# A decode kernel's wo rows over 16 DMA engines, and its value tiles taken four blocks at a time

## The chip, the core and the metric

The kernel runs on one core of one Trainium2 chip. The metric is the device time of one execution in microseconds (us); below 192.66 us is the median of three runs (192.44 to 192.67). A profile of one execution and its trace are at hand: for each engine (PE, the TensorE matmuls; PEld, its weight loads; DVE, VectorE; ACT, ScalarE; POOL, GpSimd; SP, SyncE, which here only issues DMAs) the start and length of each instruction, and for the DMA engines every packet and every semaphore increment.

## The reference

A gated mix of two branches over one token x of 512 numbers, all in bf16:

```
q = (x @ wq) as 32 heads of 128
scores = q . k_cache * 128**-0.5          # k_cache, v_cache: 32 heads x 4096 x 128
o = softmax(scores) @ v_cache
a = o (4096 numbers) @ wo                 # wo: 4096 x 512
h = relu(x @ w1 + b1) ** 2                # 1376 wide
b = h @ w2 + b2
g = sigmoid(sum(x * gate_w))
out = g * a + (1 - g) * b                 # 512 numbers
```

Each cache is 32 MiB, wq and wo 4 MiB each, w1 and w2 2.7 MiB together. Every byte is used once.

## The kernel before, in words

**Tiles.** Four heads make a tile of 4 MiB, [128 partitions x 128 blocks x 128]: 32 partitions for each head, 128 positions in a partition. There are 8 key tiles and 8 value tiles. A ring of five slots holds them; the list `LOADS` has their order (k0, k1, k2, v0, k3, v1, ... k7, v5, v6, m, v7), where m is a slot with w1, w2 and the last part of wo. SP issues the loads in that order on one queue; before each one `free` waits until the slot's old tile is used up. For a value tile this is a count on `s_pv`, one for each unit done.

**Units and steps.** A tile is worked through in four units, and all engines follow a common count of steps i = 0 to 31, one for each key unit (the loops at the end of each engine's program). In step i

- DVE multiplies 20 blocks of the key unit with q and sums them (`ttr`, line 734; 24 blocks in the last tile);
- PE transposes the other 12 blocks (`transposes`, line 516), ACT copies them out (`evac`, line 415), PE forms their scores (`scores`, line 529) one step later;
- at a tile's border ACT copies the scores of PE into S (`sc_copy`, line 422), DVE takes the maximum over each partition (`smax`, line 741), PE turns it (`max_rows`, line 536), DVE takes it over the head (`gmax`, lines 748 and 751), PE spreads it (`max_cols`, line 541), ACT forms the exponentials E (`exps`, line 434). DVE does `gmax` behind the products of the next unit; only at the border before the last tile (i = 28) it does it ahead of them.
- PE multiplies value units with E (`pv`). Which ones in which step stands in the table `PV`: unit i - 11 as a rule, from step 25 on two at a time, none in steps 28 and 29, the rest in steps 30 and 32 and after the loop. In a step they come behind the transposes and scores.

**Two forms of a value unit.** The narrow form (line 570) loads each of 32 value blocks as weights and multiplies with four columns of E: 32 matmuls, the result in the layout that is wanted. The wide form (line 562) loads 16 columns of E as weights and multiplies with four blocks (512 columns) at once: 8 matmuls. Its result is [16 x 512], of which the four diagonal 4 x 128 pieces are wanted; ACT copies it to `parts` (`parts_copy`, line 440), and PE adds the pieces to the tile's narrow result (line 576). `WIDE` says how many units of a tile are wide: three in tiles 0 to 2, none in the others.

**Norms.** `den`, `recip` and `norm` divide a group of heads (`GR`: 0 to 7, 8 to 15, 16 to 23, 24 to 27, 28 to 31) by its sums and write `onorm`. `norm` of the first two groups stands on DVE behind the products of steps 19 and 27.

**wo.** The first 28 heads' part of wo goes into W, where wq was, once q is formed (`started`): 112 rows of 32 KB (32 rows of wo each), placed on the partitions so that each DMA engine moves a chosen number of them. `FIRST` lists the rows that SP sends (three at a time), `RUNS` those that POOL sends; POOL's queue takes its engines from a cursor, and `turns` sends small dummy loads (`dm`) that move it. By these lists engines 0, 1, 2, 4, 7 and 8 move eight rows, engine 3 one, the others seven. After the last norm of head 27, `turn_a` and `spread_a` bring the outputs into W's order by the selection matrix `selA`, and `out_a` and DVE's `rows_v` multiply with W; `add_v` adds DVE's sum. The last four heads' part and w2's last rows come at the end of SP's queue (`out_b`, `mlp_out`).

Of the kernel before, what the change touches and what calls it, by code (L numbers as in the profile page):

```python
# [5 lines left out]
def bass_gated_mix__gqa_block_cached__dense_activation_squared_relu__decode_kernel(  # L6
# [15 lines left out]
    fp32 = mybir.dt.float32  # L22
# [30 lines left out]
    PV = {i: [i - LAG] for i in range(LAG, LAG + (NT - 3) * U)}  # L53
    PV[25] = [14, 15]
    PV[26] = [16, 17]
    PV[27] = [18, 19]
    for i in (28, 29, 30):
        del PV[i]
    PV[NU - 2] = [NU - 3 * U, NU - 3 * U + 1]
    PV[NU] = list(range(NU - 3 * U + 2, NU - U))  # L60
# [4 lines left out]
    NG = len(GR)  # L65

    WIDE = {0: 3, 1: 3, 2: 3}
    SLOTS = 5
    NS = 2  # L70
    NC = 2
# [3 lines left out]

    NA = 28
    NZ = NH - NA
    TS = [0, 3, NZ]

    TV = 10  # L80
# [2 lines left out]
    INNER, OUTER, SEAM = range(3)  # L83
    RUNS = [(INNER, 4, 12, 0, 2), (INNER, 4, 12, 1, 2),
            (OUTER, 4, 4, 0, 1), (OUTER, 8, 8, 0, 1), (OUTER, 4, 4, 1, 1), (OUTER, 8, 8, 1, 1),
            (OUTER, 4, 4, 2, 1), (OUTER, 8, 8, 2, 1),
            (OUTER, 3, 2, 3, 1), (SEAM, 7, 2, 3, 1)]
    FIRST = [(INNER, 0, 3, 0, 1), (INNER, 0, 3, 1, 1), (INNER, 0, 3, 2, 1), (INNER, 0, 3, 3, 1),
             (OUTER, 0, 3, 0, 1), (OUTER, 0, 3, 1, 1), (OUTER, 0, 3, 2, 1), (OUTER, 0, 3, 3, 1)]

# [15 lines left out]
    def strips():  # L106
        q = 0
        for run in RUNS + FIRST:
            yield (*place(*run), q)
            q += place(*run)[2]  # L110
        assert q == 4 * NA

    STRIPS = list(strips())

# [19 lines left out]
    with ctx:  # L134
# [11 lines left out]
        def held(kind, j=0):  # L146
            return ring[:, AT[kind, j] % SLOTS, :]
# [9 lines left out]
        W5 = W4 + NZ * DM  # L157
        wob_sb = held("m")[:, W4:W5].rearrange("p (h n) -> p h n", h=NZ)
        oA, fin4 = [held("m")[0:p, W5 + n * 128:W5 + n * 128 + 128] for n, p in enumerate((NA, 4))]
        vsum = held("k", NT - 1)[:, 0:2 * DM].bitcast(fp32)  # L160

# [23 lines left out]
        onesf = sb("onesf", [128, 128], fp32)  # L186
        qcol = sb("qcol", [128, NH], bf16)
        S = sb("S", [128, NS, B], fp32)
        parts = sb("parts", [4 * R, 512], fp32)
        E = sb("E", [128, NE, B, R], bf16)  # L190
        mp = sb("mp", [128, NT], fp32)
        gm = sb("gm", [1, 2, R], fp32)
# [35 lines left out]
        acc = pQ[:, 256:260]  # L228

        def O(a, b):  # L230
            return [pO, pO, pX, pO, pX][[n for n, g in enumerate(GR) if g[0] <= a < g[1]][0]][:, 64 + a:64 + b]

        s_x = sem("s_x")
        s_wq = sem("s_wq")
# [7 lines left out]
        s_dm = [sem(f"s_dm{n}") for n in range(len(RUNS))]  # L242
        s_wr = sem("s_wr")
        s_wk = sem("s_wk")
        s_vl = {(j, n): sem(f"s_vl{j}{n}") for j in PARTS for n in range(len(PARTS[j]) - 1)}
        s_sel = sem("s_sel")
        s_b1 = sem("s_b1")
# [29 lines left out]
        s_e = sem("s_e")  # L277
        s_pv = sem("s_pv")
        s_pt = sem("s_pt")
        s_den = sem("s_den")  # L280
        s_rd = sem("s_rd")
        s_on = sem("s_on")
# [35 lines left out]
        @block.sync  # L318
        def _(eng):
            for n, (kind, j) in enumerate(LOADS):  # L320
                free(eng, n)
                if n == SLOTS - 1:
                    started(eng)
                    for p, st, k, q in STRIPS[len(RUNS):]:
                        eng.dma_start(W[p:p + st * (k - 1) + 1:st, :], woa_v[q:q + k, :]).then_inc(s_wr, 16)
                if kind == "v" and j in PARTS:
                    for w in range(len(PARTS[j]) - 1):
                        part = slice(PARTS[j][w] * 128, PARTS[j][w + 1] * 128)
                        eng.dma_start(held("v", j)[:, part], v_v[j][:, part]).then_inc(s_vl[j, w], 16)  # L329
                elif kind in "kv":  # L330
                    eng.dma_start(held(kind, j), (k_v if kind == "k" else v_v)[j])\
                       .then_inc(s_l[n % SLOTS], 16)
                elif kind == "m":
                    eng.dma_start(held("m")[:, 0:W2], w1_v).then_inc(s_w[0], 16)
                    eng.dma_start(held("m")[:, W2:W3], w2_v).then_inc(s_w[1], 16)
            for c in range(len(TS) - 1):
                eng.dma_start(wob_sb[:, TS[c]:TS[c + 1], :], wob_v[:, TS[c]:TS[c + 1], :])\
                   .then_inc(s_wo[c], 16)
            eng.dma_start(w2b, B_w2[F - 128:F, :]).then_inc(s_w[2], 16)
            eng.wait_ge(s_f4, 1)  # L340
            eng.dma_start(out[0, 0, :].rearrange("(j p) -> j p", p=128), fin4).then_inc(s_out, 16)

        @block.gpsimd
        def _(eng):
            eng.memset(ident[:, :], 0.0).then_inc(s_id, 1)
            eng.memset(identf[:, :], 0.0).then_inc(s_id, 1)
            eng.memset(onesf[:, :], 1.0).then_inc(s_cst, 1)
            eng.wait_ge(s_id, 2)
            for m in (ident, identf):  # L350
                eng.affine_select(out=m[:, :], in_=m[:, :], compare_op=ALU.not_equal, fill=1.0,
                                  base=0, pattern=[[-1, 128]], channel_multiplier=1)\
                   .then_inc(s_id, 1)
            eng.memset(RS[:, :], 0.0).then_inc(s_cst, 1)
            eng.memset(E[:, :, :, :], 0.0).then_inc(s_cst, 1)
            eng.memset(selA[:, :, :], 0.0).then_inc(s_sel, 1)
            eng.wait_ge(s_sel, 1)
            for n, (p, st, k, q) in enumerate(STRIPS):
                eng.wait_ge(s_sel, n + 1)
                part = selA[:, :, p:p + st * (k - 1) + 1]  # L360
                eng.affine_select(out=part, in_=part, compare_op=ALU.not_equal, fill=1.0, base=-st * q,
                                  pattern=[[st, 4], [-1, st * (k - 1) + 1]], channel_multiplier=4 * st)\
                   .then_inc(s_sel, 1)

            started(eng)
            sent = 0
            for n, ((back, d), run) in enumerate(zip(turns(), RUNS)):
                if back:
                    eng.inc_swdge_sem([], [], mode="reset_dge_cursor")  # L370
                if d:
                    src = B_w1[0:d, 0:32].rearrange("p (a c) -> p a c", a=2)
                    eng.dma_start(dm[0:d, sent, :, 0:4], src[:, :, 0:4]).then_inc(s_dm[sent], 16)
                    sent += 1
                p, st, k, q = STRIPS[n]
                eng.dma_start(W[p:p + st * (k - 1) + 1:st, :], woa_v[q:q + k, :],
                              max_dma_last_dim=16384).then_inc(s_wp[n], 16)
            for n in range(sent):
                eng.wait_ge(s_dm[n], 16)
            eng.wait_ge(s_wr, 16 * len(FIRST))  # L380
            for q in s_wp[:-1]:
                eng.wait_ge(q, 16)
            eng.wait_ge(s_wp[-1], 16)
            eng.memset(tick[:, :], 0.0).then_inc(s_wk, 1)
# [3 lines left out]
        def _(eng):  # L388
# [48 lines left out]

            def parts_copy(j):
                eng.wait_ge(s_pv, U * j + WIDE[j])
                eng.activation(parts[:, :], pX[0:4 * R, :], ACT.Copy).then_inc(s_pt, 1)  # L440

            for c in range(EARLY):
                qb_copy(c)
# [17 lines left out]
        def _(eng):  # L461
# [76 lines left out]
            def max_cols(j):  # L538
# [2 lines left out]
                eng.matmul(MB[:, j:j + 1], gx[0:1, j % 2, :], onesf[0:1, 0:1],  # L541
                           start=True, stop=True).then_inc(s_mb, 1)

            def pv(u):
                j, w = u // U, u % U
                lo, hi = w * B // U, (w + 1) * B // U
# [6 lines left out]
                    landed(eng, "v", j)  # L553
                if w == 0:
                    eng.wait_ge(s_e, R * (j + 1))
                    for g in range(2, NG):
                        if u == GR[g][0]:
                            eng.wait_ge(s_on, g - 1)
                n = WIDE.get(j, 0)
                if w < n:  # L560
                    for b in range(lo, hi, 4):
# [2 lines left out]
                                        start=(b == 0), stop=(b == n * B // U - 4), skip_group_check=True)  # L564
                    mm.then_inc(s_pv, 1)
                    return
                if n and w == n and R * j == GR[1][0]:
                    eng.wait_ge(s_on, 1)
                for b in range(lo, hi):
                    mm = eng.matmul(O(R * j, R * j + R), held("v", j)[:, b * 128:(b + 1) * 128],  # L570
                                    E[:, j % NE, b, :], start=(b == n * B // U), stop=(n == 0 and b == B - 1),
                                    skip_group_check=True)
                if n and w == U - 1:
                    eng.wait_ge(s_pt, list(WIDE).index(j) + 1)
                    for b in range(4):
                        mm = eng.matmul(O(R * j, R * j + R), parts[:, b * 128:(b + 1) * 128],  # L576
                                        identf[0:4 * R, R * b:R * b + R], start=False, stop=(b == 3),
                                        skip_group_check=True)
                mm.then_inc(s_pv, 1)

            def den(c):
# [17 lines left out]
            def out_a():  # L599
                eng.wait_ge(s_ac, 2)  # L600
                for t in range(TP):
                    for j in range(4):
                        eng.matmul(acc[:, j:j + 1], wo_sb[:, t, j * 128:(j + 1) * 128], o2A[:, t:t + 1],
                                   start=(t == 0 and j == 0), stop=False, skip_group_check=True)

            def add_v():
                eng.wait_ge(s_vs, TV)
# [66 lines left out]
            spread_a()  # L674
            out_a()
            max_cols(NT - 1)
            mlp_h()
            den(NG - 1)
            for n in range(FG):
# [14 lines left out]
        def _(eng):  # L694
# [65 lines left out]
            def norm(c):  # L760
                a, b = GR[c]
                eng.wait_ge(s_rd, c + 1)
                eng.wait_ge(s_pv, b)
                eng.scalar_tensor_tensor(out=onorm[:, a:b], in0=O(a, b), scalar=gcol[:, 0:1],
                                         in1=rden[:, a:b], op0=ALU.mult, op1=ALU.mult)\
                   .then_inc(s_on, 1)
# [39 lines left out]
            for i in range(NU + 1):  # L806
# [12 lines left out]
                    qcol_copy(EARLY + i - 1)  # L819
                if i >= 12 and (i - 12) % 8 == 0 and (i - 12) // 8 < NG - 2:  # L820
                    recip((i - 12) // 8)
                if i >= LAG + 1 and (i - LAG - 1) % 8 == 7 and i < NU:
                    norm((i - LAG - 1) // 8)
            norm(NG - 2)
            smax(NT - 1)
            eng.wait_ge(s_at, 1)
# [44 lines left out]
```

## Time and profile before

| | us |
|---|---|
| median of three runs | 192.66 |
| the profiled execution: time | 192.5 |
| its span, first to last instruction | 191.1 |
| DVE busy | 158.6 |
| PE busy | 122.1 |
| ACT busy | 84.3 |
| granted TensorE clock, mean over the span | 0.674 of full |
| moved by DMA | 78.70 MB, 412 GB/s over the span |

In the lines shown below, a line of the page's section 2 is the span in 40 slices, each digit a busy share in tenths. A line of groups has source line, engine, operation, output and inputs, count, then busy time in us, mean ns, and the idle time before it with what ended it. A line of a timeline has start (us from the span's start), length in us, engine, source line, operation, output and inputs, shapes and count, and in brackets the idle time ahead and what ended it. The matmuls of one line that follow each other are merged. In the page's table of queues, a line has packets, MB and share of the DMA engines' time; "instruction" queues carry the engines' own programs.

### The profile page before, as it was taken

The numbers are of one execution on the slowest core, as the hardware profiler recorded it, in microseconds if no ns is written. First come the engines' busy times: TensorE is split into PE (matmuls) and PEld (weight loads), VectorE is DVE, ScalarE is ACT, GpSimd is POOL, SyncE is SP. The second block draws the span as 40 slices with busy tenths as digits, with TensorE's granted clock in tenths as the row PEclk, the third lists the DMA queues.
The fourth block names the chain that finished last, engine by engine and source line by source line (L and its number), as shares of the span: only waits on it lengthen the run. The fifth ranks groups of instructions, "written<-read, shape, count | busy, mean of one in ns | idle before, by whom it ended". The sixth has DMA issues, their size and how long they took to land.

```text
span 191.1 us, 5609 instructions
## 1 busy us (share of the span) xinstructions
PE 122.1 (64%) x1864; PEld 92.8 (49%) x1866; DVE 158.6 (83%) x1387; ACT 84.3 (44%) x207; POOL 18.4 (10%) x48
## 2 busy tenths in 40 slices
PE   0019764644524694898499986845876488548975
PEld 0014343534413543276256544745876277437964
DVE  0031399999999999999999999998999799998821
ACT  2013975825843654077409542943644293000400
POOL 7630000990000000000000000000000000000000
PEclk9999998555555558699859759955555555555555
DMA  6999999999999999999999999999999999999992
GB/s 219 440 440 439 439 439 430 439 398 451 432 424 405 432 406 432 442 420 439 442 427 422 425 434 425 417 424 432 425 430 435 398 424 406 419 421 426 414 388 72
DMA packets 5298, 78.70 MB, mean 412 GB/s; under 512 B 1099, under 2 KB 1741, under 8 KB 1870
## 3 DMA queue, kind: packets, MB, share of 16 engines
q1 hardware_dynamic: 4488, 75.47, 93.1%
q0 software_dynamic: 768, 2.89, 3.7%
q8 instruction: 14, 0.23, 0.5%
q14 instruction: 14, 0.11, 0.2%
q10 hardware_dynamic: 14, 0.01, 0.0%
HBM read 78.35 MB, written 0.00 MB: 410 GB/s over the span
## 4 chain that ended last, share of the span: by engine, by line
DVE 46%; DMA 38%; SPq 7%; PE 4%; ACT 2%; issue 2%; DVEq 0%; ACTq 0%
DVE ring L734 43%; DMA ring<-in_A_k_cache_dram 25%; DMA ring<-in_A_wo_dram 14%; SPq L329 6%; DVE S L734 2%; PE pX L562 2%; ACT E L434 1%; PE KP L516 1%; PE pO L576 1%; ACT kT L415 0%; DVE gm L748 0%; DVE gx L751 0%; ACT parts L440 0%; PE pQ L637 0%; DVE mp L741 0%
## 5 line engine op out<-in xcount | busy, mean ns | idle before, releaser
L734 DVE CUSTOM_DVE_ANT_0 ring<-ring,qb 128x128 bf16<-128x128 bf16 x656 | 140.6, 281 | 1.4 <-DMA ring<-in_A_k_cache_dram 1.3
L415 ACT ACTIVATE kT<-KP 128x768 bf16<-128x768 bf16 (+1 forms) x64 | 46.6, 779 | 47.1 <-PE pQ L529 19.0
L734 DVE DVE_READ_ACCUMULATOR2_ANT S<- 128x1 f32 x656 | 50.5, 77 | 0.1
L516 PE MATMUL KP<-ident,ring 128*128 128x128 bf16 x368 | 37.9, 275 | 9.5 <-DMA ring<-in_A_k_cache_dram 6.2
L516 PEld LDWEIGHTS KP<-ident,ring 128*128 128x128 bf16 x368 | 30.9, 126 | 14.1 <-DMA ring<-in_A_k_cache_dram 6.5
L562 PE MATMUL pX<-ring,E 128*16 128x512 bf16 x72 | 24.0, 493 | 0.0
L434 ACT ACTIVATE E<-S,nM 32x128 bf16<-32x128 f32 x32 | 18.6, 580 | 1.0
L570 PE MATMUL pO<-E,ring 128*128 128x4 bf16 x352 | 10.8, 166 | 4.9 <-DMA ring<-in_A_v_cache_dram 4.9
L570 PEld LDWEIGHTS pO<-E,ring 128*128 128x128 bf16 x352 | 10.2, 102 | 5.3 <-DMA ring<-in_A_v_cache_dram 5.2
L536 PE MATMUL pM<-identf,mp 128*1 128x128 f32 x8 | 3.0, 370 | 15.1 <-DVE mp L741 15.1
L562 PEld LDWEIGHTS pX<-ring,E 128*16 128x16 bf16 x72 | 6.9, 106 | 11.5 <-issue 7.7
L570 PE MATMUL pX<-E,ring 128*128 128x4 bf16 x384 | 11.3, 166 | 1.6 <-DMA ring<-in_A_v_cache_dram 1.6
L570 PEld LDWEIGHTS pX<-E,ring 128*128 128x128 bf16 x384 | 11.0, 105 | 1.8 <-DMA ring<-in_A_v_cache_dram 1.8
L426 ACT ACTIVATE nM<-pM 128x1 f32<-128x1 f32 x8 | 1.4, 174 | 19.0 <-PE pM L541 19.0
L529 PE MATMUL pQ<-qcol,kT 128*128 128x4 bf16 x176 | 7.7, 168 | 2.3 <-ACT kT L415 2.3
L541 PE MATMUL pM<-onesf,gx 1*128 1x1 f32 x16 | 4.2, 329 | 7.0 <-DVE gx L751 7.0
L529 PEld LDWEIGHTS pQ<-qcol,kT 128*128 128x128 bf16 x176 | 7.1, 105 | 3.1 <-ACT kT L415 3.1
L536 PEld LDWEIGHTS pM<-identf,mp 128*1 128x1 f32 x8 | 0.7, 85 | 16.3 <-DVE mp L741 16.1
L700 DVE CUSTOM_DVE_ANT_0 ring<-ring 1x512 bf16<-1x512 bf16 x1 | 0.7, 680 | 9.4 <-DMA ring<-in_gate_w_dram 9.4
L529 PEld LDWEIGHTS pS<-qcol,kT 128*128 128x128 bf16 x192 | 7.4, 106 | 1.7 <-issue 1.7
L434 ACT ACTIVATION_READ_ACCUMULATOR E<-S,nM 32x1 f32 x32 | 8.1, 253 | 0.0
L529 PE MATMUL pS<-qcol,kT 128*128 128x4 bf16 x192 | 7.7, 168 | 0.0
(88 smaller groups left out, 109.0 us busy)
## 6 DMA issues: line engine op xcount, KB each, us to landing
ring<-in_A_k_cache_dram SPq DMA_DIRECT2D x8, 4096.0 KB, 29.5
ring<-in_A_v_cache_dram SPq DMA_DIRECT2D x5, 4096.0 KB, 29.0
W<-in_A_wq_dram SPq DMA_DIRECT2D x1, 4096.0 KB, 12.4
ring<-in_A_v_cache_dram SPq DMA_DIRECT2D x2, 2048.0 KB, 27.7
ring<-in_A_v_cache_dram SPq DMA_DIRECT2D x4, 1024.0 KB, 27.7
ring<-in_A_v_cache_dram SPq DMA_DIRECT2D x2, 1280.0 KB, 31.9
W<-in_A_wo_dram POOLq DMA_DIRECT2D x2, 768.0 KB, 17.9
ring<-in_B_w_dram SPq DMA_DIRECT2D x1, 1376.0 KB, 25.3
```

Of the source, the lines that this page charges most:

```text
L329: eng.dma_start(held("v", j)[:, part], v_v[j][:, part]).then_inc(s_vl[j, w], 16)
L415: eng.activation(kT[:, n % NC, 0:HB[u // U] * 128], KP[n % 3][:, 0:HB[u // U] * 128], ACT.Copy).then_inc(s_ev, 1)
L426: eng.activation(nM[:, j:j + 1], MB[:, j:j + 1], ACT.Copy).then_inc(s_nm, 1)
L434: eng.activation(E[rows, j % NE, :, r], S[rows, j % NS, :], ACT.Exp, bias=nM[rows, j:j + 1], scale=SCALE, accum_out=RS[rows, R * j + r:R * ...
L516: mm = eng.transpose(KP[n % 3][:, y * 128:(y + 1) * 128], held("k", j)[:, b * 128:(b + 1) * 128], ident[:, :])
L529: mm = eng.matmul(S2[j % 2][:, c:c + R], kT[:, n % NC, y * 128:(y + 1) * 128], qcol[:, R * j:R * j + R], start=True, stop=True)
L536: eng.transpose(MT[0:1, :], mp[:, j:j + 1], identf[:, :]).then_inc(s_mt, 1)
L541: eng.matmul(MB[:, j:j + 1], gx[0:1, j % 2, :], onesf[0:1, 0:1], start=True, stop=True).then_inc(s_mb, 1)
L562: mm = eng.matmul(pX[0:4 * R, :], E[:, j % NE, b:b + 4, :].rearrange("p b r -> p (b r)"), held("v", j)[:, b * 128:(b + 4) * 128], start=(b ...
L570: mm = eng.matmul(O(R * j, R * j + R), held("v", j)[:, b * 128:(b + 1) * 128], E[:, j % NE, b, :], start=(b == n * B // U), stop=(n == 0 a ...
L576: mm = eng.matmul(O(R * j, R * j + R), parts[:, b * 128:(b + 1) * 128], identf[0:4 * R, R * b:R * b + R], start=False, stop=(b == 3), skip ...
L734: ins = eng.tensor_tensor_reduce(kb, kb, qb[:, j, :], 1.0, 0.0, ALU.mult, ALU.add, S[:, j % NS, b:b + 1])
```

## The change

1. Two of the 112 rows (64 rows of wo) leave W. `FIRST` stays; `RUNS` is written so that engine 3 moves none, engines 11 to 15 six, all others eight. The 64 rows come instead as single rows of 1 KB onto 64 partitions of slot m, in one DMA on SP's queue ahead of w1, and `out_h` multiplies them with the last norm column.
2. Tiles 0, 1, 2 and 4 are wide in all four units, tile 3 in three: 19 of the 20 units of tiles 0 to 4.
3. The parts are handled otherwise: ACT copies the four pieces by four instructions to the partitions 0, 32, 64 and 96 of a zeroed [128 x 128] `parts`, and PE adds them by one matmul with a 0/1 matrix `wanted`, at the first unit of the next tile (`add_parts`). POOL makes both tensors at the start.
4. Units 18 and 19 no longer run together in step 27: 18 in step 27, 19 in step 28. The norms of the first two groups wait for one unit more where the tile is in `WIDE`, and stand one step later on DVE. All groups but the fourth now accumulate in the same PSUM bank, pO.

```diff
     PV[26] = [16, 17]
-    PV[27] = [18, 19]
-    for i in (28, 29, 30):
+    PV[27] = [18]
+    PV[28] = [19]
+    for i in (29, 30):
         del PV[i]
...
-    WIDE = {0: 3, 1: 3, 2: 3}
+    WIDE = {0: 4, 1: 4, 2: 4, 3: 3, 4: 4}
     SLOTS = 5
...
     NZ = NH - NA
+    HR = 64
     TS = [0, 3, NZ]
...
             (OUTER, 4, 4, 0, 1), (OUTER, 8, 8, 0, 1), (OUTER, 4, 4, 1, 1), (OUTER, 8, 8, 1, 1),
-            (OUTER, 4, 4, 2, 1), (OUTER, 8, 8, 2, 1),
-            (OUTER, 3, 2, 3, 1), (SEAM, 7, 2, 3, 1)]
+            (OUTER, 4, 4, 2, 1), (OUTER, 8, 3, 2, 1),
+            (OUTER, 4, 3, 3, 1), (SEAM, 7, 2, 3, 1), (OUTER, 9, 2, 3, 1)]
     FIRST = [(INNER, 0, 3, 0, 1), (INNER, 0, 3, 1, 1), (INNER, 0, 3, 2, 1), (INNER, 0, 3, 3, 1),
...
             q += place(*run)[2]
-        assert q == 4 * NA
+        assert q == 4 * NA - HR // 32
...
         oA, fin4 = [held("m")[0:p, W5 + n * 128:W5 + n * 128 + 128] for n, p in enumerate((NA, 4))]
+        woh_sb = held("m")[128 - HR:128, W5 + 256:W5 + 256 + DM]
         vsum = held("k", NT - 1)[:, 0:2 * DM].bitcast(fp32)
...
         S = sb("S", [128, NS, B], fp32)
-        parts = sb("parts", [4 * R, 512], fp32)
+        parts = sb("parts", [128, 128], fp32)
+        wanted = sb("wanted", [128, R], fp32)
         E = sb("E", [128, NE, B, R], bf16)
...
         def O(a, b):
-            return [pO, pO, pX, pO, pX][[n for n, g in enumerate(GR) if g[0] <= a < g[1]][0]][:, 64 + a:64 + b]
+            return (pX if GR[3][0] <= a < GR[3][1] else pO)[:, 64 + a:64 + b]
...
         s_wk = sem("s_wk")
+        s_wh = sem("s_wh")
         s_vl = {(j, n): sem(f"s_vl{j}{n}") for j in PARTS for n in range(len(PARTS[j]) - 1)}
...
         s_pt = sem("s_pt")
+        s_wt = sem("s_wt")
         s_den = sem("s_den")
...
                 elif kind == "m":
+                    eng.dma_start(woh_sb, A_wo[NA * 128 - HR:NA * 128, :]).then_inc(s_wh, 16)
                     eng.dma_start(held("m")[:, 0:W2], w1_v).then_inc(s_w[0], 16)
...
                    .then_inc(s_sel, 1)
+            eng.memset(parts[:, :], 0.0).then_inc(s_wt, 1)
+            eng.memset(wanted[:, :], 0.0).then_inc(s_wt, 1)
+            for b in range(4):
+                eng.wait_ge(s_wt, 2 + b)
+                eng.affine_select(out=wanted[:, :], in_=wanted[:, :], compare_op=ALU.not_equal, fill=1.0,
+                                  base=-(32 + R) * b, pattern=[[-1, R]], channel_multiplier=1).then_inc(s_wt, 1)
...
                 eng.wait_ge(s_pv, U * j + WIDE[j])
-                eng.activation(parts[:, :], pX[0:4 * R, :], ACT.Copy).then_inc(s_pt, 1)
+                if j == 0:
+                    eng.wait_ge(s_wt, 6)
+                for b in range(4):
+                    eng.activation(parts[32 * b:32 * b + 4 * R, :], pX[0:4 * R, b * 128:(b + 1) * 128], ACT.Copy)                       .then_inc(s_pt, 1)
...
+            def normed(j):
+                g = [n for n, g in enumerate(GR) if g[0] == R * j]
+                if g and g[0] not in (0, 3):
+                    eng.wait_ge(s_on, min(g[0], 3))
+            def add_parts(j):
+                eng.wait_ge(s_pt, 4 * (j + 1))
+                if WIDE[j] == U:
+                    normed(j)
+                eng.matmul(O(R * j, R * j + R), parts[:, :], wanted[:, :], start=(WIDE[j] == U), stop=True,
+                           skip_group_check=True)
             def pv(u):
...
                     eng.wait_ge(s_e, R * (j + 1))
-                    for g in range(2, NG):
-                        if u == GR[g][0]:
-                            eng.wait_ge(s_on, g - 1)
+                    if j - 1 in WIDE:
+                        add_parts(j - 1)
                 n = WIDE.get(j, 0)
...
                     return
-                if n and w == n and R * j == GR[1][0]:
-                    eng.wait_ge(s_on, 1)
+                if w == n:
+                    normed(j)
                 for b in range(lo, hi):
...
                                     skip_group_check=True)
-                if n and w == U - 1:
-                    eng.wait_ge(s_pt, list(WIDE).index(j) + 1)
-                    for b in range(4):
-                        mm = eng.matmul(O(R * j, R * j + R), parts[:, b * 128:(b + 1) * 128],
-                                        identf[0:4 * R, R * b:R * b + R], start=False, stop=(b == 3),
-                                        skip_group_check=True)
                 mm.then_inc(s_pv, 1)
...
                                    start=(t == 0 and j == 0), stop=False, skip_group_check=True)
+            def out_h():
+                eng.wait_ge(s_wh, 16)
+                for j in range(4):
+                    eng.matmul(acc[:, j:j + 1], woh_sb[:, j * 128:(j + 1) * 128], onorm[128 - HR:128, NA - 1:NA],
+                               start=False, stop=False, skip_group_check=True)
...
             max_cols(NT - 1)
+            out_h()
             mlp_h()
...
                 eng.wait_ge(s_rd, c + 1)
-                eng.wait_ge(s_pv, b)
+                eng.wait_ge(s_pv, b + (b // R - 1 in WIDE))
                 eng.scalar_tensor_tensor(out=onorm[:, a:b], in0=O(a, b), scalar=gcol[:, 0:1],
...
                     recip((i - 12) // 8)
-                if i >= LAG + 1 and (i - LAG - 1) % 8 == 7 and i < NU:
-                    norm((i - LAG - 1) // 8)
+                if i >= LAG + 2 and (i - LAG - 2) % 8 == 7 and i < NU:
+                    norm((i - LAG - 2) // 8)
             norm(NG - 2)
...
```

## The prediction

> **What bounds the kernel now.** The page was read first: the slices of DMA, of the granted TensorE clock and of PE, then the groups.
>
> ```profile
> PE   0019764644524694898499986845876488548975
> PEclk9999998555555558699859759955555555555555
> DMA  6999999999999999999999999999999999999992
> ...
> q8 instruction: 14, 0.23, 0.5%
> ...
> L734 DVE CUSTOM_DVE_ANT_0 ring<-ring,qb 128x128 bf16<-128x128 bf16 x656 | 140.6, 281 | 1.4 <-DMA ring<-in_A_k_cache_dram 1.3
> ```
>
> The 16 DMA engines are busy from 5 us to the last slice: transfers are the first bound. DVE, in its key products, has waited for a key tile 1.3 us in all: it is a second bound that the first hides by a hair. TensorE has the full clock only now and then, and none after 124 us. The q8 line is TensorE's own instructions, fetched in 14 packets of 16 KB by the same DMA engines.
>
> Next, the trace's semaphore increments, one for each DMA engine, show who finishes last. For the last load (w2b) they come at 185.7 (one engine), 186.6 to 187.3 (seven) and 188.3 to 188.8 (eight), mean 187.65. A 32 KB row takes an engine 1.22 us; a q8 packet took 0.97 to 1.10 us, in which its engine moved nothing else. So rows and instruction packets make the spread, and perfect balance is worth at most 188.8 - 187.65 = 1.15 us.
>
> Then the timeline of PE, where the value units run:
>
> ```profile
> 94.94 3.58 PE L562 MATMUL pX<-ring,E 128*16 128x512 bf16 x8
> ...
> 100.62 1.89 PE L562 MATMUL pX<-ring,E 128*16 128x512 bf16 x8
> ...
> 106.82 3.10 PE L562 MATMUL pX<-ring,E 128*16 128x512 bf16 x8
> ...
> 132.78 1.04 PE L570 MATMUL pO<-E,ring 128*128 128x4 bf16 x32
> ...
> 136.12 0.58 PE L541 MATMUL pM<-onesf,gx 1*128 1x1 f32 x2 [0.70 <-DVE gx L751]
> 136.64 1.87 PE L570 MATMUL pO<-E,ring 128*128 128x4 bf16 x64
> ...
> 141.08 1.87 PE L570 MATMUL pX<-E,ring 128*128 128x4 bf16 x64 [0.98 <-DMA ring<-in_A_v_cache_dram]
> ...
> 144.41 1.85 PE L570 MATMUL pX<-E,ring 128*128 128x4 bf16 x64
> 146.12 0.46 PE L529 MATMUL pS<-qcol,kT 128*128 128x4 bf16 x12
> ```
>
> A narrow unit (32 matmuls, L570) takes about 0.9 us at either clock. A wide one (8 matmuls of 512 columns, L562) takes 1.89 us at the full clock and 3.5 us at half. The wide form saves instructions and costs TensorE time. The last line is the last scores of key tile 6. What hangs on it is in the timeline of DVE:
>
> ```profile
> 148.92 0.28 DVE L741 TENSOR_REDUCE mp<-S 128x1 f32<-128x128 f32 x1
> 149.67 0.28 DVE L748 TENSOR_REDUCE gm<-pM 1x4 f32<-1x128 f32 x1 [0.47 <-PE pM L536]
> 149.99 0.21 DVE L751 TENSOR_SCALAR gx<-gm 1x128 f32<-1x128 f32 x1
> 150.84 0.29 DVE L734 CUSTOM_DVE_ANT_0 ring<-ring,qb 128x128 bf16<-128x128 bf16 x1 [0.65 <-DMA ring<-in_A_k_cache_dram]
> ```
>
> At this one tile border the maximum (L741 to L751) stands on DVE ahead of the next tile's products, not behind them. Scores that come late here stop DVE. And the end of PE's timeline:
>
> ```profile
> 184.41 1.21 PE L570 MATMUL pX<-E,ring 128*128 128x4 bf16 x40
> 186.27 1.44 PE L570 MATMUL pX<-E,ring 128*128 128x4 bf16 x48 [0.65 <-DMA ring<-in_A_v_cache_dram]
> 188.27 0.56 PE L637 MATMUL pQ<-onorm,ring 128*128 128x1 bf16 x16 [0.56 <-DMA ring<-in_A_wo_dram]
> ```
>
> PE waits 0.65 us there for the last value tile: the compute chain may be 0.65 us later before it moves the end.
>
> **The change part by part.** *Instructions.* Ten units turn from 32 matmuls to 8 (-240). The 24 matmuls that add the parts (12 in the code, two each) become 10, and the 64 single rows add 4. From 1864 matmuls that leaves 1614. The 14 packets came about every 129 weight loads; 1616/129 gives 12. Two packets less are 2 x 1.03 us on two of 16 engines.
>
> *Rows.* I joined the packets of an engine end to start. The engine that is last, 188.8, is then the one with a single row and DVE's instruction packets (8 KB, 0.33 us, and the packet behind each 0.65 us longer): engine 3. It loses its row, -1.22. Six engines got two q8 packets each, and five of them are, as I read it, 11 to 15: -1.22 each. Of engines 5, 6, 9 and 10 (+1.22), three ended near 187 and come to about 188.4; one may be the sixth that was hit twice, and loses one packet. One of engines 0 to 2 ended near 188.4 and keeps its eight rows. The single rows add four 1 KB packets to every engine, 42 ns apart at the end of the trace: +0.17. New last engine: 188.4 + 0.17 = 188.6. Gain 0.2 us; bounds: 1.15 (balance) and -0.2 (the engine near 188.64 keeps its place).
>
> *Hidden.* POOL gets two memsets (0.20 each), four selects and one more (0.28 to 0.43), ahead of its 21.65 us wait before L373. Its DMAs go from 7 dummies and 10 runs to 6 and 11, 0.6 us of issue each, ending at 43 us; the rows are needed at 172.87 (L595) and landed by 99.6. Without that cover the whole tail would wait for rows. SP issues one DMA more at 148.8, 0.4 us, and everything behind it 0.4 us later; the last value tile then waits for unit 19, which moves behind step 28, so its issue goes from 149.7 to about 156. Its data start near 177, 20 us of queue later. Were that gone, each us late would be a us of idle DMA. The first normalisation moves one step on, and waits for a unit that has run by then; the second (0.15 us) moves from before L741 to behind the 24 products of step 28, and unit 20 now waits for it. It is there at about 157.6; PE reaches unit 20 later.
>
> *Tiles 0 to 2.* The fourth unit goes from 0.95 us, a wait of 0.59 and 1.05 us of adding (86.79) to 1.89 and one two-pass matmul later, about 0.4. No loss; PE waits 2.1 to 2.7 us for DVE at those borders anyway.
>
> *Tiles 3 and 4* have no such cover. By starts, from PE's timeline:
> - Unit 13: 3.56 at half clock against 0.91: +2.65. The wait of 0.70 at L541 goes: unit 14 starts +1.95, at 138.6.
> - Unit 14 at full clock, as at 100.62: +1.0; transposes and scores behind it at full clock: -0.55 (0.68 against 1.23). PE is then at tile 4's door at 142.5. It was there at 140.1 and waited 0.98 for the value tile, so +1.4 of 141.08.
> - The parts of tile 3: ACT's exponentials end 1.95 later, at 141.3. Four copies follow; the row nearest to 16x128 is the exponential of 32x128, a next step after 0.33: 1.3 in all. PE waits till 142.7, adds 0.4: unit 16 starts at 143.1, +2.0. (Bounds for the copies: 0.59, the one copy of now, and 4 x 0.59.)
> - Units 16 and 17: 3.74 against 1.73: +4.0. Transposes -0.55. Unit 18 alone, 1.87, against 18 and 19, 1.71: +3.6.
>
> So the last scores of tile 6 start at 149.7. From their start to DVE's next product lie 1.38 (copies of S, ended 147.50) + 1.28 (148.92 to 150.20) + 0.04 = 2.7 us; the key tile allows 150.84, so 148.1 was allowed: DVE loses 1.6 us. At the end: +0.15 (the moved normalisation), -0.36 (DVE's wait at 172.0 for unit 27 goes), +0.12 (four more matmuls; 40 take 1.20 at L628), -0.65 (PE's wait for data). Sum +0.86. The DMA gain lies beside it and is lost.
>
> The profiled execution took 192.5 (span 191.1 and 1.4 around it), 0.16 under the median. 192.5 + 0.86 = 193.4.
>
> **A rule against the row.** Windows at 1.53 us modulo 3.41 hold every change of the granted clock in the trace, and the clock rose after windows filled to 80% or more by transposes and wide units. The window view has PE 8.90 us busy of the 10 from 136 to 146 at a granted clock of 0.50. *The Trainium skill, TensorE: Matmul & The Clock Gate, Part 1, has the clock come after one window of about 3.4 us of activity and go after an idle one. Taken by busy time it would have had PE at full clock here, which the 0.50 contradicts. That the windows run freely of the kernel, as it says, one trace can't show; it would spread the times of the runs.*
>
> **The rivals.** (1) Full clock from unit 13 on. Wide units cost 1.87 throughout and the transposes 0.55 less each; PE then waits for the parts till 140.8, and the scores start near 148.1, as allowed. DVE loses 0.1, its end stays inside the 0.65, and DMA decides: 192.5 - 0.2 = 192.3, no change to be told. For it: after the wide unit at 100.62 the clock stayed up for 4.9 us. Against: it falls in each gap like PE's 4.38 us wait at 131. *This is also what the skill's rule, taken by busy time, would give.* (2) The rows bite: as (1), but my engine in 0 to 2 is lighter than read, and the last landing nears the mean. PE's 0.65 caps it: 191.85 to 192.1, and it decides only if the scores start before 148.1. (3) The clock falls between units 14 and 16, in 3 us of light work, as it fell at 107.3 inside the unit at 106.82: units 16 to 18 lose up to 1.2 to 1.7, DVE 3.0: 192.5 + 2.3 = 194.8.
>
> **How the numbers follow.** Forecast case 0.40 (192.8 to 193.9 by the copies' bounds and window phase), rival (1) 0.25, (2) 0.20, (3) 0.15. Two runs of this kernel differ by about 0.2%, 0.39 us, without cause: a time from 192.27 to 193.05 is no change. Rival (2) is faster: 0.20. Rival (1) and the edge of the forecast case: 0.28. The rest, slower: 0.52. The range takes in (2)'s body and (3): 192.0 to 194.8.
>
> **What would show it.** q8 with 12 packets; 1614 matmuls; wide units at L562's new line near 3.5 once after 132 and 1.9 after; the scores before the border near 149.7 and DVE waiting on L741 for S or PE rather than for the key tile; the last products of DVE ending near 173; the last landing near 188.6 and PE not waiting for the last value tile. If DVE's product starts at 150.9 again, the step on units 13 to 18 is wrong; if the last landing moves over 0.5 us, the step on rows is.

## The result, and the profile after

| | before | after |
|---|---|---|
| median, us | 192.69 | 194.03 (193.85 to 194.66) |
| ratio | 1 | 1.0074 [1.0058, 1.0090] |
| the profiled execution, us | 192.5 | 194.06 |
| span, us | 191.1 | 192.7 |
| last landing of the last load (w2b), us | 188.80 | 190.36 |
| mean landing over the 16 engines, us | 187.65 | 187.84 |
| latest engine above the mean, us | 1.15 | 2.53 |

Slower by 0.74%, where +0.37% was forecast. The page of after, its slices, its queue of TensorE's instructions and the group of DVE's key products:

```profile
PE   0019765644524693898469866999699688749865
PEclk9999995755555558699996997599879785555555
DMA  6999999999999999999999999999999999999980
...
q8 instruction: 12, 0.20, 0.4%
...
L764 DVE CUSTOM_DVE_ANT_0 ring<-ring,qb 128x128 bf16<-128x128 bf16 x656 | 140.7, 282 | 0.6 <-DMA ring<-in_A_k_cache_dram 0.6
```

The 12 packets are there as forecast. TensorE has the full clock much longer than before (0.753 of full over the span, against 0.674). The last load lands at 190.36, in the middle of the last slice of DMA, and that slice is 0: one engine of 16 doesn't show on this line. The timeline of PE over the wide units that were to make it late (start, length, engine and line):

```profile
132.43 1.89 PE L591 MATMUL pX<-ring,E 128*16 128x512 bf16 x8
...
137.22 2.50 PE L591 MATMUL pX<-ring,E 128*16 128x512 bf16 x8
...
142.37 3.62 PE L591 MATMUL pX<-ring,E 128*16 128x512 bf16 x16
...
146.98 1.89 PE L591 MATMUL pX<-ring,E 128*16 128x512 bf16 x8
148.81 0.45 PE L546 MATMUL pS<-qcol,kT 128*128 128x4 bf16 x12
```

Unit 13 ran at the full clock (132.43: 1.89, forecast 3.56), unit 14 in part at half (137.22: 2.50, forecast 1.89), and the last scores of key tile 6 start at 148.81, not 149.7. What DVE made of it, in its timeline:

```profile
150.20 0.29 DVE L771 TENSOR_REDUCE mp<-S 128x1 f32<-128x128 f32 x1 [0.60 <-ACT S L436]
150.85 0.28 DVE L778 TENSOR_REDUCE gm<-pM 1x4 f32<-1x128 f32 x1 [0.36 <-PE pM L553]
151.17 0.21 DVE L781 TENSOR_SCALAR gx<-gm 1x128 f32<-1x128 f32 x1
151.31 0.29 DVE L764 CUSTOM_DVE_ANT_0 ring<-ring,qb 128x128 bf16<-128x128 bf16 x1
```

The first product of tile 7 starts at 151.31; before it was 150.84. DVE does wait for S and PE now, as forecast, but loses 0.47 us and not 1.6. Its last maximum (L771 of the last tile, the end of its key work) comes at 172.41, 0.27 after before's 172.14. And the end of PE's timeline:

```profile
184.88 1.21 PE L599 MATMUL pO<-E,ring 128*128 128x4 bf16 x40
...
187.79 1.44 PE L599 MATMUL pO<-E,ring 128*128 128x4 bf16 x48 [1.71 <-DMA ring<-in_A_v_cache_dram]
...
189.84 0.56 PE L666 MATMUL pQ<-onorm,ring 128*128 128x1 bf16 x16 [0.61 <-DMA ring<-in_A_wo_dram]
```

PE waits 1.71 us for the last value tile where it waited 0.65. So the end came from the transfers, 1.56 later, and not from a late TensorE. The landings of w2b, from the trace's semaphore increments, each engine against the mean:

```
before  -1.94 -1.03 -0.92 -0.81 -0.74 -0.70 -0.55 -0.39 +0.64 +0.72 +0.77 +0.87 +0.95 +0.99 +0.99 +1.15
after   -2.70 -1.31 -0.87 -0.82 -0.68 -0.12 -0.04 +0.04 +0.21 +0.22 +0.30 +0.70 +0.75 +0.87 +0.92 +2.53
```

One engine is 1.6 us behind all others. Joining each engine's packets end to start shows what it carried: eight rows of wo, one q8 packet at 93.9, and the last q8 packet at 184.98. In that last packet it went from 1.09 above the mean to 2.54, by the landings of the loads before and behind it. As joined in this trace, the q8 packets go round eight engines (called the ring below), packet n and n + 8 on the same one. Four of the eight are of the kind with six rows, four of the kind with eight. With 12 packets, four engines get two.

### The profile page after: what moved, and what is told of

Same layout as the page of the kernel before. It is cut to its first block, busy times and chain, and to the rows that moved or that the text cites. A ratio compares the mean times of both kernels' runs of the same rounds, so it can differ in the third digit from the quotient of the medians.

```text
span 192.7 us, 5144 instructions
## 1 busy us (share of the span) xinstructions
PE 128.4 (67%) x1616; PEld 86.0 (45%) x1616; DVE 158.6 (82%) x1387; ACT 88.1 (46%) x224; POOL 19.7 (10%) x55
## 4 chain that ended last, share of the span: by engine, by line
DVE 51%; DMA 26%; PE 16%; SPq 3%; issue 2%; ACT 1%; DVEq 0%
DVE ring L764 47%; DMA ring<-in_A_wo_dram 15%; DMA ring<-in_A_k_cache_dram 11%; PE pX L591 9%; SPq L336 3%; PE KP L533 3%; DVE S L764 2%; ACT S L436 1%; DVE gm L778 1%; PE pM L558 1%; DVE gx L781 1%; PE pQ L546 1%; ACT parts L457 1%; PE pS L546 0%; PE pO L599 0%
## 5 line engine op out<-in xcount | busy, mean ns | idle before, releaser
L591 PE MATMUL pX<-ring,E 128*16 128x512 bf16 x152 | 43.8, 442 | 0.0
L533 PE MATMUL KP<-ident,ring 128*128 128x128 bf16 x368 | 34.9, 260 | 5.5 <-ACT kT L429 3.0
L533 PEld LDWEIGHTS KP<-ident,ring 128*128 128x128 bf16 x368 | 28.5, 119 | 12.4 <-issue 5.3
L591 PEld LDWEIGHTS pX<-ring,E 128*16 128x16 bf16 x152 | 13.5, 98 | 20.2 <-issue 8.6
L599 PE MATMUL pO<-E,ring 128*128 128x4 bf16 x288 | 8.5, 166 | 1.7 <-DMA ring<-in_A_v_cache_dram 1.7
L599 PEld LDWEIGHTS pO<-E,ring 128*128 128x128 bf16 x288 | 8.4, 105 | 2.6 <-DMA ring<-in_A_v_cache_dram 1.8
L558 PEld LDWEIGHTS pM<-onesf,gx 1*128 1x128 f32 x16 | 3.1, 244 | 10.0 <-DVE gx L781 9.9
```

Source lines behind the costliest of these rows:

```text
L533: mm = eng.transpose(KP[n % 3][:, y * 128:(y + 1) * 128], held("k", j)[:, b * 128:(b + 1) * 128], ident[:, :])
L591: mm = eng.matmul(pX[0:4 * R, :], E[:, j % NE, b:b + 4, :].rearrange("p b r -> p (b r)"), held("v", j)[:, b * 128:(b + 4) * 128], start=(b ...
```

## The experiments

Three theories. **1**, the prediction's: the late TensorE holds DVE, and DVE's end sets the end. **2a**: the dealing of the rows to the engines does it; the eighth row went to engines that also take TensorE's instruction packets, and one that gets two of them is last. **2b**: the 64 single rows do it, by more than the 0.17 forecast.

All runs in one table; landings from each run's own profiled execution, times in us. The ratio, with its 95% interval in brackets, isn't taken from the medians shown:

| kernel | median | ratio to before | profiled | mean landing | last landing | engines over 1.9 above the mean |
|---|---|---|---|---|---|---|
| before | 192.7 | | 192.50 | 187.65 | 188.80 | 0 |
| after | 194.03 | 1.0074 [1.0058, 1.0090] | 194.06 | 187.84 | 190.36 | 1 |
| rows only | 194.20 | 1.0086 [1.0073, 1.0099] | 194.25 | 188.12 | 190.55 | 4 |
| wide units only | 192.65 | 1.0005 [0.9996, 1.0013] | 192.93 | 187.51 | 189.09 | 0 |
| seven rows, first try | 194.30 | 1.0075 [1.0057, 1.0092] | 194.94 | 188.35 | 191.23 | 1 |
| unit 18 later | 194.42 | 1.0109 [1.0077, 1.0141] | 194.14 | 187.93 | 190.32 | 3 |
| after, seven rows | 193.12 | 1.0023 [1.0014, 1.0032] | 193.52 | 187.94 | 189.54 | 0 |
| before, dealt as after | 193.46 | 1.0043 [1.0030, 1.0055] | 193.45 | 187.58 | 189.75 | 2 |
| before, single rows added | 193.34 | 1.0035 [1.0023, 1.0047] | 193.34 | 188.30 | 189.59 | 0 |
| after, no single rows | 193.45 | 1.0033 [1.0015, 1.0050] | 193.83 | 187.33 | 189.98 | 4 |
| before, 9 and 10 with eight | 193.40 | 1.0040 [1.0027, 1.0052] | 193.40 | 187.66 | 189.71 | 2 |
| after once more | 194.21 | 1.0080 [1.0065, 1.0096] | 194.06 | 187.90 | 190.35 | 4 |

In all twelve traces the profiled time is the last landing plus 3.69 to 3.98 us, while the last landing itself moves over 2.43 us. The end follows the last landing, which speaks for the transfers.

**The two halves of the change.** Rows only, on the kernel before:

```
+            (OUTER, 4, 4, 2, 1), (OUTER, 8, 3, 2, 1),
+            (OUTER, 4, 3, 3, 1), (SEAM, 7, 2, 3, 1), (OUTER, 9, 2, 3, 1)]
...
+                    eng.dma_start(woh_sb, A_wo[NA * 128 - HR:NA * 128, :]).then_inc(s_wh, 16)
...
+            out_h()
```

> The kernel before with the row step alone: 110 rows of wo's first part spread as in the changed kernel, 64 single rows, their four matmuls; the value tiles as before. Theory 1 (the late TensorE sets the end): the row step is worth 0.2 at most, 192.3 to 192.8. Theory 2 (the DMA engines set the end: one engine with eight rows takes a second packet of PE's instructions and its last packets land 1.6 us behind the next engine's): with the 14 packets of before, of which the last few fall on engines by the ring's position, the last landing may lie anywhere from 188.6 to 190.4, so 192.3 to 194.1; what decides is whether the latest engine is one with eight rows and two such packets.

And the value units only: the changed kernel with the row step taken back, by these lines against it:

```
-    HR = 64
+    HR = 0
...
-            (OUTER, 4, 4, 2, 1), (OUTER, 8, 3, 2, 1),
-            (OUTER, 4, 3, 3, 1), (SEAM, 7, 2, 3, 1), (OUTER, 9, 2, 3, 1)]
+            (OUTER, 4, 4, 2, 1), (OUTER, 8, 8, 2, 1),
+            (OUTER, 3, 2, 3, 1), (SEAM, 7, 2, 3, 1)]
...
-                    eng.dma_start(woh_sb, A_wo[NA * 128 - HR:NA * 128, :]).then_inc(s_wh, 16)
...
-            out_h()
```

> The changed kernel with the row step undone: 112 rows as before, no single rows; the 19 wide units, the four-strip parts and the new order of the units stay. Theory 1: DVE still waits at the border of key tile 6 and most of the loss stays, 193.6 to 194.2. Theory 2: the engines with the seam's rows carry six to eight rows as before, the 12 packets fall on other weights; last landing 188.6 to 189.2 and 192.4 to 193.0 if no eight-row engine takes two packets late, near 194 if one does.

Rows only: 194.20, above theory 1's 192.8 and 0.1 above theory 2's range. Wide units only: 192.65, no change to be told, inside theory 2's range and far below theory 1's 193.6. The whole loss is in the row step. In the trace of the wide units alone DVE waits as long for S as in after (0.61 us), and its last maximum comes at 172.43. PE's timeline shows where that is hidden:

```profile
186.57 1.44 PE L597 MATMUL pO<-E,ring 128*128 128x4 bf16 x48 [0.68 <-DMA ring<-in_A_v_cache_dram]
```

PE still waits 0.68 for data. Theory 1 falls for the time, though its stall exists.

**Unit 18 behind the border's scores**, with the rows as changed:

```
-    PV[27] = [18]
-    PV[28] = [19]
+    PV[28] = [18, 19]
```

> The changed kernel with value unit 18 moved from step 27 to step 28, behind the scores of the border, so that TensorE reaches the last scores of key tile 6 one wide unit earlier (1.9 to 3.6 us). The rows stay as changed. Theory 1: DVE's idle 0.60 at the border of step 28 goes and the time falls by 0.3 to 1.0, to 193.0 to 193.7. Theory 2: DVE's end doesn't set the end, the last load does: 193.8 to 194.2.

The stall was to go. Instead it grew, for units 13, 16 and 17 met half clock in part (3.38 us for unit 13, 5.26 for 16 and 17 together). DVE's timeline, and then PE's:

```profile
151.16 0.28 DVE L770 TENSOR_REDUCE mp<-S 128x1 f32<-128x128 f32 x1 [2.49 <-ACT S L435]
...
174.74 0.27 DVE L770 TENSOR_REDUCE mp<-S 128x1 f32<-128x128 f32 x1
```

```profile
187.20 2.49 PE L598 MATMUL pO<-E,ring 128*128 128x4 bf16 x88
...
190.07 0.59 PE L665 MATMUL pQ<-onorm,ring 128*128 128x1 bf16 x16 [0.39 <-DVE onorm L793]
```

DVE ends 2.33 later than in after and PE no longer waits for the value tile, yet the execution took 194.14 against 194.06: last landings of 190.32 and 190.36. So DVE may be about 2 us late before it moves this end. The run doesn't give theory 1's price cleanly, since the edit and the clock moved together; that its median is 0.4 above after's, with one execution of 196.29, may be DVE showing through there; no trace shows that.

**Seven rows, first try.**

```
+            (OUTER, 4, 4, 2, 1), (OUTER, 8, 7, 2, 1),
+            (OUTER, 4, 1, 3, 1), (SEAM, 7, 2, 3, 1)]
```

> The changed kernel with its 110 rows dealt otherwise: seven on DMA engines 5, 6 and 9 to 14, six on 15, eight on 0, 1, 2, 4, 7 and 8, none on 3. Everything else stays, the late TensorE too. Theory 1: no change, 193.8 to 194.2. Theory 2: the engine that takes the second packet has seven rows, 1.2 us less, so the last landing falls from 190.36 to about 189.2 and the time to 192.7 to 193.1.

It missed: 194.30. The edit wasn't what it was meant to be. Its trace holds sixteen packets of 2 KB on POOL's queue that no other trace has: the run of a single row was cut over all 16 engines, POOL's cursor would then be back at 4 instead of 5, and by the cursor's rule the next two rows would go to engines 6 and 7. That these were the engines isn't shown. One engine at 1.56 above the mean was hit by the q8 packet at 176.0 and went to 3.00. Beside that, 32 KB packets took 1261 ns on average from 80 to 100 us in this execution, where the other eleven traces have 1219 to 1226; its mean landing is later for that and not for the rows.

**Seven rows without a single-row run**, on the changed kernel:

```
+            (OUTER, 4, 4, 2, 1), (OUTER, 8, 8, 2, 1),
+            (SEAM, 7, 2, 3, 1)]
```

> The changed kernel with its 110 rows dealt so that the engines which take PE's instruction packets have no eighth row: eight rows on engines 0, 1, 2, 7 and 8, seven on 4, 5, 6 and 9 to 15, none on 3, with no run of a single row. (In the run with seven rows on 5, 6 and 9 to 14, the run of one row was cut into sixteen packets of 2 KB, so the two rows behind it went to engines 6 and 7 and not to 7 and 8.) Theory 2a (the eighth row on engines that take two packets costs 1.2 to 1.6): last landing 189.0 to 189.4, 192.7 to 193.1. Theory 2b (the 64 single rows are what costs): no change, 193.8 to 194.3.

193.12, last landing 189.54: 0.91 us of the loss gone by where the rows lie, with the single rows and the wide units kept. The time is 0.02 above theory 2a's range, the landing 0.14, and both far from 2b's. What is left above before is 0.44.

**The dealing alone, on the kernel before.**

```
+            (OUTER, 4, 4, 2, 1), (OUTER, 8, 5, 2, 1),
+            (OUTER, 4, 3, 3, 1), (SEAM, 7, 2, 3, 1), (OUTER, 9, 2, 3, 1)]
```

> The kernel before with its 112 rows dealt much as in the changed kernel (eight on 0, 1, 2 and 4 to 10, seven on 11 and 12, six on 13 to 15, none on 3), without any single rows, and with the value tiles as before. Theory 2a: mean landing of the last load as before, 187.6, but the latest engine 2.1 to 2.5 above it, 189.8 to 190.1, so 193.5 to 193.9. Theory 2b: no change, 192.4 to 192.8.

193.46, +0.78, just under theory 2a's range. The mean landing is that of before (187.58 against 187.65), the latest engine 2.17 above it. So 2b alone falls.

**Two rows moved.**

```
+            (OUTER, 4, 4, 2, 1), (OUTER, 8, 6, 2, 1),
+            (OUTER, 3, 2, 3, 1), (SEAM, 7, 2, 3, 1), (OUTER, 9, 2, 3, 1)]
```

> The kernel before with two of its 112 rows moved: engines 9 and 10 get an eighth row, 14 and 15 go down to six. Nothing else. Theory 2a (an engine with eight rows and two instruction packets ends 1.0 to 1.3 above one with seven and two): the latest engine 2.0 to 2.5 above the mean of 187.65, 189.6 to 190.1, and 193.3 to 193.9; where neither 9 nor 10 is hit twice in an execution, 192.4 to 192.8. If the ring of the packets goes on from execution to execution (14 packets over 8 engines), both kinds of execution may show. Rival (only the number of rows moved counts, or only the dealing as a whole): a quarter of the 0.8 of the full dealing or less, 192.6 to 192.9.

193.40, +0.67: two rows out of 112, moved from engines 14 and 15 to 9 and 10, cost nearly as much as the whole dealing. Two engines stand out, at 1.96 and 2.05. The rival of a quarter of 0.8 or less falls. It isn't how many rows move that counts, but that an engine gets eight rows and two packets.

**The single rows alone, on the kernel before.**

```
+                    eng.dma_start(woh_sb, A_wo[NA * 128 - HR:NA * 128, :]).then_inc(s_wh, 16)
                     eng.dma_start(held("m")[:, 0:W2], w1_v).then_inc(s_w[0], 16)
```

> The kernel before, with the load of the 64 single rows added ahead of w1 (TensorE waits for it; nothing uses it, all 112 rows stay). Forecast's price: four 1 KB packets for each engine, 0.17, so 192.8. Price read off the traces: the packets beside them grow from 416 to as much as 519 ns while single rows are written, 0.3 to 0.5 for every engine, so 192.9 to 193.2.

193.34, +0.66, more than either price; the mean landing rises by 0.65 while the spread stays (1.29). The window view from 161 to 176 us, first of before, then with the single rows (columns: window, busy time of PE, its weight loads, DVE, ACT and POOL with counts, granted clock, DMA share, GB/s):

```profile
161.00:166.00 5.00, 3.34 (x105) 3.18 (x103) 5.00 (x47) 0.57 (x3) 0.00 (x0) 0.50 1.01 418
166.00:171.00 5.00, 1.79 (x61) 1.62 (x59) 5.00 (x49) 0.00 (x0) 0.00 (x0) 0.50 1.02 425
```

```profile
161.00:166.00 5.00, 3.69 (x113) 3.44 (x109) 5.00 (x49) 1.84 (x6) 0.00 (x0) 0.50 1.01 421
166.00:171.00 5.00, 2.02 (x64) 1.86 (x64) 5.00 (x49) 0.00 (x0) 0.00 (x0) 0.50 1.02 387
```

The engines stay busy, but move 387 GB/s in the five microseconds of the single rows, where before has 425 and the run that only deals anew 415. After shows the same:

```profile
166.00:171.00 5.00, 2.16 (x69) 1.91 (x67) 5.00 (x49) 0.00 (x0) 0.00 (x0) 0.50 1.04 391
```

By packets: a single row took 48 ns, four for an engine, 0.19. The 128 packets of 11,008 bytes of w1 behind them took 456 ns in this run, where they took 416 before: eight for an engine, 0.31. The 8 KB packets beside them lost 0.11 more. Sum 0.61 of the 0.65. All seven traces with single rows have 453 to 464 for w1's packets, the other five 416 to 421. Why the packets beside them grow while 1 KB packets are written isn't settled.

**The changed kernel without the single rows.**

```
-                    eng.dma_start(woh_sb, A_wo[NA * 128 - HR:NA * 128, :]).then_inc(s_wh, 16)
...
-            out_h()
```

> The changed kernel without the load of the 64 single rows and without their four matmuls: those 64 rows of wo are left out of the result. Dealing of the 110 rows as changed. Theory 2a: the mean falls by 0.3 to 0.5, the latest engine stays 2.4 to 2.5 above it, 193.4 to 193.8. Theory 2b: 192.4 to 192.7.

Mean landing 187.33, 0.51 under after's; four engines 2.17 to 2.65 above it, so 193.83 in the profile. But two of its twelve executions took 191.99 and 192.14, under before, and the others 193.24 to 193.98. That is what 2a gives if the ring doesn't begin each execution at the same engine: with 12 packets four of eight engines are hit twice, and now and then they are the four light ones. No trace of such an execution was kept. With 14 packets six of eight are hit twice and some heavy engine always is: the dealing alone took 193.43 to 193.60 in every execution.

**The changed kernel once more**, without an edit:

> The changed kernel once more. If the ring's place differs from execution to execution, the number of engines that end over 2 above the mean differs from the one of the first profile (there it was one), between none and four, and the time follows the latest landing plus 3.7: 193.8 to 194.7. If the ring stands still, the same one engine is late, at 2.5 above the mean.

The same time, 194.06, but four engines late (2.19 to 2.45) instead of one. The ring's place does differ between executions of one program, and this trace shows the packets at work. Of its loads that land from 149 us on, those ahead of the q8 packet at 167.20 have no engine over 1.9 us above their mean. Behind the packets at 167.20, 173.36, 180.24 and 186.37 it is one, two, three and four engines.

The lengths of the q8 packets bear the ring out in the other traces too. From the third packet on, packets eight apart differ by 4 ns in the median over the twelve traces, those one to seven apart by 13 to 43. So a length tells a place in the ring:

```
after             1048 1086 1086 1016 1018 1081 1078 1061 1099 1109 1086 1016
after once more    962  982 1071 1078 1068 1108 1099 1086 1031 1018 1073 1081
```

The lengths 1099, 1109, 1086, 1016 of after's packets 9 to 12 stand three packets earlier in the second row, at 6 to 9 (1108, 1099, 1086, 1031): the ring began elsewhere. The last four packets of the second row give the places of the four late engines. By the best fit of the pattern, 1, 4, 3, 2 and 4 of these four places are hit twice in after, rows only, unit 18 later, before dealt as after, and after without single rows. Those are the numbers of late engines in the table.

DVE's last maximum came at 173.31 here, 0.90 later than in the first profile, without moving the time.

## Why the prediction was right or wrong

The sign was right and the time 0.6 us off the forecast, by the wrong step: that is luck. The loss that was forecast for DVE didn't reach the end, and the rows, forecast as a hidden gain of 0.2, made the loss. No kernel's median beat the kernel before; the wide units alone equal it.

- **Units 13 to 18 and DVE's 1.6 us**, the term that made the +0.86: wrong for the time. The stall is real and of the kind foretold (L771 waits for S, L778 for PE), but it was 0.47, since unit 13 met the full clock. Over seven traces with the wide units DVE's last maximum lies between 172.11 and 175.44 (before: 172.14), so a lateness of the forecast's size does occur. It is no mark of the wide units: the four runs that keep the old units and touch the rows alone have it at 172.96 to 173.57. And the wide units alone cost 0.04 us by the medians, -0.08 to +0.25 by the ratio's interval.
- **"PE not waiting for the last value tile"**: wrong; it waited 1.71. The cover of 0.65 was taken as fixed. It is the gap between the transfers and DVE, and the same change that made DVE later made the transfers later.
- **Rows, new last landing 188.6**: this is the step that failed. It came to 190.36, beyond the 0.5 us that the prediction set as its own test. Two terms of it were wrong. First, I took the six engines that had two packets in one trace for a property of the engines, "11 to 15" for five of them, and gave the extra rows to engines that "ended near 187". Engines 5, 6, 9 and 10 stand in the ring too (late engines appear where they get an eighth row and go where they don't), and which of the ring's eight get two differs from execution to execution. By the pattern of lengths two of the six hit twice in the trace before were of these four places, where the prediction allowed for one. Eighth rows there cost 0.67 to 0.78 us with 14 packets. Second, the single rows: +0.17 in the sum, +0.65 measured on the mean landing, for I priced their own packets and not what the others lose beside them.
- **The sum now**, from the parts measured on the kernel before: dealing +0.78, single rows +0.66, wide units +0.04 make +1.48; measured +1.34 and +1.48 in the two sets of runs of the changed kernel. The dealing was measured with 112 rows and 14 packets, so the sum is an estimate: rows only cost +1.59, where its two parts make +1.44.
- **Instructions**: 12 packets, as forecast; 1616 matmuls against 1614. But "two packets less" freed no engine that mattered.
- **The parts' copies**: four copies took 1.13 us, against 1.3.
- **Rivals**: (1) and (2) had the right bound, the transfers, and the wrong sign, for both rested on the same reading of the ring. Units 16 to 18 met no fall of the clock as in (3) in after; in the run with unit 18 later 16 and 17 did, and even so the end moved by 0.08.
- **The rule weighed there**: the changes of the granted clock lie at 1.84 us modulo 3.41 and at 0.14, 1.70 apart, in the two profiled executions of the same changed kernel. *That agrees with the Trainium skill, TensorE: Matmul & The Clock Gate, Part 1, which lets the windows run freely of the kernel; the prediction could only leave it open.* The spread that it was to make may be in DVE's last maximum (172.41 and 173.31 in these two); both took 194.06, since DVE doesn't set the time.

## What to carry to other kernels

Where transfers bound a kernel to the last microsecond, balance them by what each DMA engine really carries, the instruction packets of the compute engines among it, and not by one trace: repeat the profile before an engine is called light. Price a small transfer by what its neighbours lose beside it, from a window's GB/s, not by its own packets alone. And a cover seen at the end ("PE waits 0.65") belongs to two chains; ask of each part of a change which of the two it moves.

## What the runs showed of the hardware

- TensorE's instruction packets (16 KB, 0.95 to 1.24 us, in which the engine moves nothing else, as far as its packets could be joined) went round eight of the 16 DMA engines, and the place in the round differs between executions of one program: one late engine in one, four in the other, with the same dealing. Two packets on an engine that also has an eighth row put it 1.96 to 2.65 us above the mean (2.87 in the first try of seven rows).
- 64 rows of 1 KB, 0.08% of the bytes, slowed the 11 KB packets around them by some 9% (416 to 456 ns) and cost an engine 0.65 us on average.
- A load of one 32 KB partition row from POOL's queue was cut into sixteen packets of 2 KB, where rows of longer runs go as packets of 16 KB.
